# Eight blocks keep their GELU output instead of six, spread over the second pass; stored blocks are loaded into tiles that are already used

## The chip, the cores and the metric

The kernel runs on one core of one Trainium2 chip. The metric is the device time of one execution in microseconds (us). Before the change three runs gave 1454.07, 1455.67 and 1457.65 us: a median of 1455.67.

## The reference

A ConvNeXt-V2 block on one image of 512 x 512 pixels with 96 channels (C), in bf16: a depthwise 3x3 convolution, a normalisation over channels, a product up to 384 channels (E), GELU, a global response normalisation (GRN) whose scale needs the sum of squares of every one of the 384 channels over the whole image, and a product back to 96 channels with the input added.

```python
xp = jnp.pad(x, ((0,0),(pad,pad),(pad,pad),(0,0)))
out = jnp.zeros_like(x)
for i in range(K):
    for j in range(K):
        out = out + xp[:, i:i+H, j:j+W, :] * dw[i, j][None, None, None, :]
h = _layernorm(out, axis=-1)
h = jnp.einsum('bhwc,ce->bhwe', h, w1)
h = _gelu(h)
gx = jnp.sqrt((h * h).sum(axis=(1, 2), keepdims=True) + 1e-6)
nx = gx / (gx.mean(axis=-1, keepdims=True) + 1e-6)
h = grn_gamma * (h * nx) + grn_beta + h
h = jnp.einsum('bhwe,ec->bhwc', h, w2)
return x + h
```

The sums over the whole image split the work into two passes: the scale of the second product is known only when the GELU of every pixel has been seen once.

## The kernel before

**Blocks.** The image is cut into 128 blocks of 4 rows (`NBLK`). A block's GELU output g has 2048 pixels by 384 channels, 1.5 MB, in four quads of 512 pixels; one quad is turned out by one ScalarE GELU of 128 x 1536 from three PSUM banks (`banks3` gives two such sets in turn, so PE can be one quad ahead).

**Phase 1** takes the blocks in order: convolution (PE), statistics and normalisation, the normalised block `yn` to DRAM and back into a ring of six tiles `ynT`, then the first product and GELU, and the squares of g for the GRN sums. Up to block 113 the convolution of later blocks runs beside that; blocks 114 to 127 (`TAIL0` on) are turned out alone, by `mlp_tail` (L677), one after another.

The squares are taken in two ways. A quad in channel layout (`cm_unit`, three matmuls with the weights standing, channels on partitions) is squared by three VectorE statistics (`entry`, BATCH_NORM_STATS2 of 128 x 512). A quad in pixel layout (`px_unit`, pixels on partitions) is squared on PE: each half quad gives six gram matmuls of 128 x 128, g against itself, whose diagonal is added up. Grams are queued in a list and handed out by `gram_next` after each quad, one or two half quads at a time, so they run some quads later than the GELU they read. `cm_quads` says how many quads of a block take the first way. Only g in channel layout can be used by the second product.

**How phase 2 gets a block's g.** Four kinds of blocks:

- stored (`whole`, 35 of them): all four quads in channel layout, g written to DRAM in phase 1 and loaded again in phase 2 into one of two tiles `gl`
- held (`HELD`, six: 114, 116, 118, 120, 122, 125): all four quads in channel layout, g simply stays on chip
- `KEPT` (123, 124, 126, 127): recomputed, their `ynT` is still in the ring
- the others: recomputed; `ynT` is loaded again with three DMAs of 128 KB on SP's queue

So 87 blocks are recomputed (`made_q`): 12 matmuls of 128 x 512 and four GELUs each, into one of three tiles `gr`.

**Where the tail's g lies.** Held blocks 114 to 122 take the five tiles of the pool `g`, 125 the tile `gh`. Of the others, 115 to 124 go by turns into two views, `overs`, laid over the input tiles (`xin`) and the transposed input tiles (`xt`) of the convolution, which are used up by then; 126 and 127 go into `gr`.

**Between the phases** the last grams and statistics are summed, VectorE works out the scale and multiplies it into W2 (`W2s`), while the first quads are already being recomputed.

**Phase 2** goes through `ORDER`. `stage_mm2` makes a block's second product in four sub-tiles: 12 matmuls of 128 x 96 each, then VectorE adds the bias from PSUM, and after every second sub-tile the input `xr`. After each sub-tile `pace` (L372) issues recompute matmuls for blocks ahead: at least what the sub-tile after next reads, else an even share with a lead of `LEAD` = 6 quads, never more than three tiles `gr`, and never beyond the five blocks (`PRE`) whose loads have been issued.

```python
soon = (n, sub + 2) if sub < NSUB - 1 else (n + 1, 1)
due = sum(1 for v in todo if v < soon or v[0] < n)
even = LEAD + (n * NSUB + sub + 1) * total / (NSUB * NBLK)
advance(max(due, even), n + PRE)
```

At the start of block n, `load_xr` (POOL's queue) asks for the input of block n + 4 and `load_rest` for what block n + 5 needs: `ynT` on SP's queue, stored g on POOL's. Outputs leave on SP's queue, a block later. The order begins (K kept in the ring, H held, W stored, r recomputed)

```
K123 K124 K126 H114 K127 r1 W0 r2 r4 H116 r5 r6 W3 r8 r9 H118 r11 r12 W7 ...
```

and ends `... W110 r119 r121 W113`; the held blocks are at places 3, 9, 15, 21, 28 and 34.

Of the kernel before, what the change touches and what calls it, by code (L numbers as in the profile page):

```python
# [12 lines left out]
GR = 4  # L13
# [2 lines left out]
NEWTON_ITERS = 2  # L16
FILL = (6, 15)
BATCH = 4
NHELD = 6
WHOLE = (0, 3, 7)  # L20
NTAIL = 14
GRB = 3
# [34 lines left out]
def kernel(  # L57
# [25 lines left out]

    QW = GR * 128
    NQ = GR * W // QW
# [2 lines left out]
    r_dram = dram.tile([NBLK, GR, W], bf16, name="r_dram")  # L88

    TAIL0 = NBLK - NTAIL  # L90
    HELD = [NBLK - 6 - 2 * i for i in range(NHELD - 1)][::-1] + [NBLK - 3]
    KEPT = [NBLK - 5, NBLK - 4, NBLK - 2, NBLK - 1]

    def is_held(q):
        return q in HELD

    def is_whole(q):
        return q < TAIL0 and q % 10 in WHOLE
# [8 lines left out]
    whole = [q for q in range(NBLK) if is_whole(q)]  # L107
    g_dram = dram.tile([len(whole), 128, NQ * NCH * QW], bf16, name="g_dram")
# [4 lines left out]
    PXP = GR * W // 128  # L113
    MB = W // PXP
# [18 lines left out]
    consts = ctx.enter_context(tc.tile_pool(name="consts", bufs=1))  # L133
# [3 lines left out]
    dw9 = consts.tile([9, C], bf16, name="dw9")  # L137
    eye32 = consts.tile([128, 32], bf16, name="eye32")
    rowsel = consts.tile([128, GR], bf16, name="rowsel")
    w1_raw = consts.tile([C, E], bf16, name="w1_raw")  # L140
    w1p = consts.tile([128, E], bf16, name="w1p")
    w1s = consts.tile([128, E], bf16, name="w1s")
    Wq = consts.tile([128, NI, 3, GR, 32], bf16, name="Wq")
    w2_sb = consts.tile([128, NCH, C], bf16, name="w2_sb")
    gam_bf = consts.tile([128, NCH], bf16, name="gam_bf")
    bet_bf = consts.tile([128, NCH], bf16, name="bet_bf")
# [13 lines left out]
    NYT = 6  # L160
# [3 lines left out]

    W2s = consts.tile([128, NCH, C], bf16, name="W2s")
    B2c = consts.tile([128, C], f32, name="B2c")
    free = [[q for q in range(NBLK) if is_whole(q)], list(HELD)]
    free = [v for i, q in enumerate(free[0]) for v in (free[1][i:i + 1] + [q])]
    made_q = KEPT + [q for q in range(NBLK) if not is_whole(q) and not is_held(q) and q not in KEPT]
    ORDER = []  # L170
    for i, q in enumerate(made_q):
        ORDER.append(q)
        while len(ORDER) - i - 1 < (i + 1) * len(free) // len(made_q):
            ORDER.append(free[len(ORDER) - i - 1])
    assert sorted(ORDER) == list(range(NBLK))
    nth_made = {q: n for n, q in enumerate(made_q)}
    SLOTS = [q % NYT for q in KEPT + [NBLK - 6, NBLK - 3]]

    class late:
        pass  # L180
# [2 lines left out]
    pspool = ctx.enter_context(tc.tile_pool(name="ps", bufs=1, space=bass.MemoryType.PSUM))  # L183
    PS = pspool.tile([128, 8, W], f32, name="PS")
    p2 = ExitStack()
    SL = PXP + 2
    with ExitStack() as p1:
        pe, dve, act, pool, sp = (InOrder(tc, e) for e in (nc.tensor, nc.vector, nc.scalar, nc.gpsimd, nc.sync))
        bstpool = p1.enter_context(tc.tile_pool(name="bst", bufs=2))
# [19 lines left out]
            return PS[:, 7 - out_banks[0] % 2, :GPS * C].rearrange("p (g c) -> p g c", g=GPS)  # L209

        Y3 = PS[:, 4:7, :]
        pc = p1.enter_context(ExitStack())
        xinpool = pc.enter_context(tc.tile_pool(name="xin", side="right", bufs=1))
        xin_all = xinpool.tile([128, 4, SL, C], bf16, name="xin")
        xins = {}

        def shift(h, j):
# [21 lines left out]
        g_setup = gpool.tile([128, NQ, NCH, QW], bf16, name="g")[:].rearrange("p t j w -> p (t j w)")  # L239
        Wd = g_setup[:, :NI * 9 * 32].rearrange("p (i k c) -> p i k c", i=NI, k=9)  # L240
        dwx = g_setup[:9, NI * 9 * 32:NI * 9 * 32 + NI * GR * 32].rearrange("p (i q c) -> p i q c", i=NI, q=GR)
        zrow = consts.tile([128, W], bf16, name="zrow")
        dve.memset(zrow[:], 0.0)
        warm = consts.tile([32, 32], bf16, name="warm")
        dve.memset(warm[:], 0.0)
# [1 line left out]
        for b in range(min(2, NBLK)):  # L247
# [3 lines left out]
                       in_=zrow[:, None, :NI * GR * 32].to_broadcast([128, 3, NI * GR * 32]), func=ACTF.Identity)  # L251
# [4 lines left out]
        for q in range(GR):  # L256
            dve.tensor_copy(out=eye32[32 * q:32 * q + 32, :], in_=ident_f[32 * q:32 * q + 32, 32 * q:32 * q + 32])

        cen = consts.tile([C, 128], bf16, name="cen")
        xtpool = pc.enter_context(tc.tile_pool(name="xt", side="right", bufs=1))  # L260
        ypool = pc.enter_context(tc.tile_pool(name="ybf", side="right", bufs=13))
        ysqpool = pc.enter_context(tc.tile_pool(name="ysq", side="right", bufs=3))
        small = pc.enter_context(tc.tile_pool(name="small", side="right", bufs=2))
        rtpool = pc.enter_context(tc.tile_pool(name="rt", side="right", bufs=2))
        rbcpool = pc.enter_context(tc.tile_pool(name="rbc", side="right", bufs=3))
        ynpool = pc.enter_context(tc.tile_pool(name="yn", side="right", bufs=3))
        NXT = 5
        xt_ring = []
        xt_all = xtpool.tile([128, NXT, NI, SL * MB], bf16, name="xT")
        for i in range(NXT):  # L270
            xt_ring.append(xt_all[:, i])
        assert NXT * NI * SL * MB >= NQ * NCH * QW
        assert 4 * SL * C >= NQ * NCH * QW
        overs = [v.rearrange("p a b c -> p (a b c)")[:, :NQ * NCH * QW].rearrange("p (t j w) -> p t j w", t=NQ, j=NCH)
                 for v in (xt_all[:], xin_all[:])]
        NS = BATCH * GR * NG
        cap = 2048 // (C * 4)
# [1 line left out]
        NSUB = PXP // GPS  # L279

        def load_xr(n, pq):
            q = ORDER[n]
            r0 = q * GR
            xr = late.xr.tile([128, PXP, C], bf16, name="xr")
            pq.dma_start(out=xr[:], in_=x[0, r0:r0 + GR].rearrange("r w c -> (r w) c").rearrange(  # L285
                "(p g) c -> p g c", g=PXP))
            grp.setdefault(q, {})["xr"] = xr

        def load_rest(n, sq, pq):
            q = ORDER[n]  # L290
            v = grp.setdefault(q, {})
            if is_held(q):
                v["g"] = gs[q]
            elif is_whole(q):
                v["g"] = late.gl.tile([128, NQ, NCH, QW], bf16, name="gl")
                pq.dma_start(out=v["g"][:].rearrange("p t j w -> p (t j w)"), in_=g_dram[whole.index(q)])
            else:
                ynt = yn_ring[SLOTS[nth_made[q] % NYT]]
                if q not in KEPT:
                    read_spread(sq, ynt, q)  # L300
                v["ynt"], v["w1"] = ynt, w1p if q in KEPT else w1s

# [54 lines left out]
        PRE = 5  # L357
        XPRE = 4
        LEAD = 6
        todo = [(n, t) for n in range(NBLK) if ORDER[n] in nth_made for t in range(NQ)]  # L360
        total = len(todo)
        made, used = [0], [0]
# [9 lines left out]
        def pace(n, sub):  # L372
            soon = (n, sub + 2) if sub < NSUB - 1 else (n + 1, 1)
            due = sum(1 for v in todo if v < soon or v[0] < n)
            even = LEAD + (n * NSUB + sub + 1) * total / (NSUB * NBLK)
            advance(max(due, even), n + PRE)

        SG = PS[:, 7, :]
# [286 lines left out]
        gs = {}  # L665
# [9 lines left out]
            dve.bn_stats(out=bsts[k][:, j, e, :], in_=gs[b][:, m, j, :])  # L675

        def mlp_tail(b, get):  # L677
            if b == HELD[-1]:
                gs[b] = late.gh.tile([128, NQ, NCH, QW], bf16, name="gh")[:]
            elif is_held(b) or b < HELD[0]:  # L680
                gs[b] = gpool.tile([128, NQ, NCH, QW], bf16, name="g")[:]
            elif b > HELD[-1]:
                gs[b] = late.gr.tile([128, NQ, NCH, QW], bf16, name="gr")[:]
            else:
                overs.append(overs.pop(0))
                gs[b] = overs[0]
# [124 lines left out]
        for k, (b0, n) in enumerate(BATCHES):  # L811
# [16 lines left out]
            for b in range(b0, b0 + n):  # L828
# [4 lines left out]
                m = s + (3 if ramp else 4)  # L833
# [10 lines left out]
        for s in range(last_slot + 1):  # L844
# [71 lines left out]
            else:  # L916
                b = mlp[0]
# [57 lines left out]
            if s == last_slot - 3:  # L975
                pc.close()
                late.gr = p2.enter_context(tc.tile_pool(name="gr", side="right", bufs=GRB))
                late.gh = p2.enter_context(tc.tile_pool(name="gh", side="right", bufs=1))
                late.xr = p2.enter_context(tc.tile_pool(name="xr", side="right", bufs=5))
                late.gl = p2.enter_context(tc.tile_pool(name="gld", side="right", bufs=2))  # L980
                late.o = p2.enter_context(tc.tile_pool(name="o", side="right", bufs=6))
            if s == last_slot - 2:
                for n in range(XPRE):
# [52 lines left out]
    with p2:  # L1036
        def out_part(q, o_sb, v):
            r0 = q * GR
            nc.sync.dma_start(
                out=out[0, r0:r0 + GR].rearrange("r w c -> (r w) c").rearrange("(p g) c -> p g c", g=PXP)[:, v],  # L1040
                in_=o_sb[:, v])

        held = None
        FIRST = 8
        for n, q in enumerate(ORDER):
            sq, pq = (sp, pool) if n < FIRST else (nc.sync, nc.gpsimd)
            if n + XPRE < NBLK:
                load_xr(n + XPRE, pq)
            if n + PRE < NBLK:
                load_rest(n + PRE, sq, pq)  # L1050
            if n == NBLK - 1:
                stage_out(*held)
                held = None
            o_sb = stage_mm2(n, q)
            if held:
                stage_out(*held)
            held = (q, o_sb)
# [30 lines left out]
```

## Time and profile before

| | |
|---|---|
| median of the three runs | 1455.67 us |
| the profiled execution, its own time | 1458.11 us |
| its span in the trace | 1456.3 us |
| granted TensorE clock, mean | 0.995 |
| ScalarE busy | 1399.4 us, 96% |
| PE matmul busy | 1388.1 us, 95% |
| VectorE busy | 1317.4 us, 90% |
| GpSimd (POOL) busy | 901.7 us, 62% |
| data moved by DMA | 421.26 MB |
| first GELU of block 115 | 881.48 us |
| last GELU of block 127 begins (row of eight from 940.62) | about 950 us |
| last GELU of phase 2 ends | 1446.84 us |

PE is TensorE's matmuls, PEld its weight loads, DVE is VectorE, ACT is ScalarE, POOL is GpSimd, SP issues DMAs. A row of the timeline gives start and length in us, engine, line, operation, what is written from what (partitions x elements), and how many such instructions are merged; in brackets how long the engine had been idle and what ended that. Almost every instruction carries line 35, that of a helper which records the instructions, so rows are told apart by their tiles: `PS<-ynT,w1s` is recompute, `PS<-W2s,...` the second product, `bst<-...` a statistic, `PS<-xin` with 128 x 128 a gram. [...]

### The profile page before, as it was taken

How to read it: one execution, taken by the hardware profiler on the slowest of the kernel's cores; microseconds unless marked ns; L12 is line 12 of the kernel's file. 1: busy time of each engine (PE TensorE's matmuls, PEld its weight loads, DVE VectorE, ACT ScalarE, POOL GpSimd, SP SyncE). 2: the span in 40 equal slices, each digit the busy share in tenths (PEclk: the TensorE clock that was granted, in tenths of full speed). 3: DMA queues.
4: the chain of work that ended last, by engine and by line, in shares of the span. 5: the costliest groups of instructions: out<-in, count | busy, mean ns of one | idle time of the engine just before them, and what ended most of it. 6: DMA issues, size and time to landing. Idle time of an engine off the chain costs nothing.

```text
span 1456.3 us, 54718 instructions
## 1 busy us (share of the span) xinstructions
PE 1388.1 (95%) x23128; PEld 812.0 (56%) x23128; DVE 1317.4 (90%) x2422; ACT 1399.4 (96%) x1591; POOL 901.7 (62%) x796
## 2 busy tenths in 40 slices
PE   8889999999999999999999998899999999999998
PEld 3444444444444444444444445567777677777776
DVE  7749999999999999999999998778888788888887
ACT  6879999999999999999999999999999899999997
POOL 2559999999999999999899998201111111111110
PEclk9999999999999999999999999999999999999999
DMA  6478889898888988988889876649999999999997
GB/s 195 153 216 234 251 262 278 265 265 260 266 258 270 269 255 269 274 252 267 248 271 274 247 242 204 185 174 371 363 336 368 394 379 415 386 412 413 405 415 307
DMA packets 167275, 421.26 MB, mean 289 GB/s; under 512 B 34198, under 2 KB 83798, under 8 KB 162550
## 3 DMA queue, kind: packets, MB, share of 16 engines
q1 hardware_dynamic: 151508, 313.80, 67.5%
q0 software_dynamic: 14960, 103.82, 18.5%
q8 instruction: 181, 2.97, 0.9%
q14 instruction: 64, 0.52, 0.1%
q10 hardware_dynamic: 562, 0.15, 0.0%
HBM read 261.38 MB, written 156.22 MB: 287 GB/s over the span
## 4 chain that ended last, share of the span: by engine, by line
PE 37%; DVE 36%; ACT 10%; DMA 8%; POOL 4%; issue 3%; SPq 1%; ACTq 0%; POOLq 0%; DVEq 0%
PE PS L35 37%; DVE bst L35 26%; DVE xT L35 7%; ACT g L35 5%; DMA ynT<-yn_dram 3%; DMA yn_dram<-yn 2%; DMA out_dram<-o_sb 2%; ACT y_bf L35 2%; POOL yn L35 2%; ACT gr L35 1%; SPq L35 1%; DVE y_bf L35 1%; POOL ysq L35 1%; DVE o_sb L35 1%; ACT xT L35 1%
## 5 line engine op out<-in xcount | busy, mean ns | idle before, releaser
L35 ACT ACTIVATE g<-PS 128x512 bf16<-128x512 f32 (+2 forms) x1046 | 707.7, 835 | 10.3 <-PE PS L35 6.5
L35 DVE BATCH_NORM_STATS2 bst<-g 128x6 f32<-128x512 bf16 x1086 | 659.0, 672 | 23.5 <-ACT g L35 23.3
L35 ACT ACTIVATE gr<-PS 128x1536 bf16<-128x1536 f32 x356 | 493.1, 1451 | 13.1 <-PE PS L35 8.0
L35 POOL TENSOR_TENSOR yn<-y_bf,rbc 128x1536 bf16<-128x1536 bf16 x126 | 391.3, 3107 | 48.8 <-ACT rbc L35 23.3
L35 PE MATMUL PS<-xT,Wq 64*32 64x511 bf16 (+1 forms) x9198 | 346.1, 389 | 16.8 <-ACT y_bf L35 4.5
L35 PE MATMUL PS<-ynT,w1p 128*128 128x512 bf16 x1170 | 335.4, 382 | 25.4 <-ACT g L35 5.4
L35 DVE TENSOR_TENSOR o_sb<-PS,B2c 128x384 bf16<-128x384 f32 x512 | 280.6, 556 | 70.1 <-PE PS L35 63.6
L35 POOL TENSOR_TENSOR ysq<-y_bf 128x1536 bf16<-128x1536 bf16 x114 | 313.3, 2748 | 26.0 <-ACT y_bf L35 17.8
L35 PE MATMUL PS<-ynT,w1s 128*128 128x512 bf16 x996 | 269.1, 379 | 5.5 <-DMA ynT<-yn_dram 3.3
L285 POOL DMA_DIRECT2D xr<-in_x_dram x116 | 62.2, 537 | 297.9 <-DVE o_sb L35 297.9
L35 PEld LDWEIGHTS <-gr 128*128 128x128 bf16 x4248 | 208.7, 98 | 56.4 <-issue 0.7
L35 PE MATMUL PS<-W2s,gr 128*128 128x96 bf16 x4176 | 218.8, 206 | 0.5 <-DVE o_sb L35 0.4
L35 PEld LDWEIGHTS <-Wq 64*32 64x32 bf16 x9216 | 113.4, 90 | 179.8 <-issue 135.1
L35 ACT ACTIVATE y_bf<-PS 128x1536 bf16<-128x1536 f32 (+2 forms) x135 | 182.4, 1357 | 18.2 <-PE PS L35 18.1
L35 PEld LDWEIGHTS <-w1p 128*128 128x128 bf16 x1170 | 90.4, 98 | 181.1 <-issue 111.5
L35 DVE STREAM_TRANSPOSE xT<-xin 128x576 f32<-128x576 f32 (+1 forms) x256 | 181.5, 748 | 6.5 <-PE PS L35 6.5
L35 DVE TENSOR_TENSOR o_sb<-o_sb,xr 128x768 bf16<-128x768 bf16 x256 | 142.8, 558 | 8.9
L35 PEld LDWEIGHTS <-g 128*128 128x128 bf16 (+1 forms) x1611 | 98.7, 98 | 84.8 <-issue 54.8
L35 PE MATMUL PS<-w1p,ynT 128*128 128x256 bf16 (+2 forms) x828 | 125.8, 272 | 9.7 <-ACT g L35 2.7
L35 PE MATMUL PS<-g 128*128 128x128 bf16 x1368 | 115.3, 221 | 1.2 <-DVE PS L35 1.2
L35 PEld LDWEIGHTS <-w1s 128*128 128x128 bf16 x996 | 79.5, 98 | 46.0 <-issue 5.5
L35 PEld LDWEIGHTS <-gl 128*128 128x128 bf16 x1680 | 82.5, 98 | 23.1 <-issue 0.9
(115 smaller groups left out, 754.9 us busy)
## 6 DMA issues: line engine op xcount, KB each, us to landing
xin<-in_x_dram SPq DMA_DIRECT2D x126, 432.0 KB
g_dram<-g SPq DMA_DIRECT2D x105, 512.0 KB
gl<-g_dram POOLq DMA_DIRECT2D x35, 1536.0 KB, 9.3
yn_dram<-yn SPq DMA_DIRECT2D x512, 96.0 KB
ynT<-yn_dram SPq DMA_DIRECT2D x128, 384.0 KB
out_dram<-o_sb SPq DMA_DIRECT2D x127, 384.0 KB
xr<-in_x_dram POOLq DMA_DIRECT2D x124, 384.0 KB, 7.5
ynT<-yn_dram SPq DMA_DIRECT2D x249, 128.0 KB
```

Source lines behind the costliest of these rows:

```text
L35: r = f(*a, **k)
L285: pq.dma_start(out=xr[:], in_=x[0, r0:r0 + GR].rearrange("r w c -> (r w) c").rearrange("(p g) c -> p g c", g=PXP))
```

## The change

- Held blocks are eight: 114, 115, 117, 118, 120, 121, 124 and 125. `KEPT` is 122, 123, 126, 127. 85 blocks are recomputed; 116 and 119 are the two of the tail that need `ynT` again.
- The two tiles `gl` are gone. The pools of the convolution's `xin` and `xt` tiles stay open to the end; some constants of the convolution move to a pool that closes with it.
- The tail's g: 114 lies over `xt`; 116, 119 and 121 lie over `xin`, one after another (121 stays); 115, 117, 118, 120 and 122 take tiles of `g`; 123 and then 124 take the tile of 122 (`gs[b] = gs[b - 1]`); 125 takes `gh`; 126 and 127 `gr`.
- A stored block is loaded into the tile of 114 or of 115, by turns. `user` names the block that must have been through the second product first; while it has not, the load is put off (`ahead`) to a later turn of the loop.
- Held blocks are spread over the order, which begins `K122 H114 K123 K126 H115 K127 r1 W0 r2 r4 W3 r5 r6 W7 ...` and ends `... r111 r112 W113 r116 r119 H125`; they are at places 1, 4, 25, 46, 67, 88, 109 and 127.
- The lead of `pace` falls in a straight line from 6 quads at the start to 3 (`LAST_LEAD`) at the end.

```diff
-    HELD = [NBLK - 6 - 2 * i for i in range(NHELD - 1)][::-1] + [NBLK - 3]
-    KEPT = [NBLK - 5, NBLK - 4, NBLK - 2, NBLK - 1]
+    HELD = [TAIL0 + i for i in (0, 1, 3, 4, 6, 7, 10, 11)]
+    KEPT = [NBLK - 6, NBLK - 5, NBLK - 2, NBLK - 1]
+    IN_XT, IN_XIN, IN_GH = TAIL0, TAIL0 + 7, TAIL0 + 11
...
-    free = [[q for q in range(NBLK) if is_whole(q)], list(HELD)]
-    free = [v for i, q in enumerate(free[0]) for v in (free[1][i:i + 1] + [q])]
+    free, rest = HELD[:2], HELD[2:]
+    for i, q in enumerate(whole):
+        free.append(q)
+        if (i + 1) * len(HELD[2:]) // len(whole) > len(HELD[2:]) - len(rest):
+            free.append(rest.pop(0))
+    assert not rest
...
-        while len(ORDER) - i - 1 < (i + 1) * len(free) // len(made_q):
+        while len(ORDER) - i - 1 < ((i + 1) * len(free) + len(made_q) // 2) // len(made_q):
...
             elif is_whole(q):
-                v["g"] = late.gl.tile([128, NQ, NCH, QW], bf16, name="gl")
-                pq.dma_start(out=v["g"][:].rearrange("p t j w -> p (t j w)"), in_=g_dram[whole.index(q)])
+                v["g"] = gs[HELD[in_order.index(q) % 2]]
+                pq.dma_start(out=v["g"].rearrange("p t j w -> p (t j w)"), in_=g_dram[whole.index(q)])
...
+        LAST_LEAD = 3
+        in_order = [q for q in ORDER if is_whole(q)]
+        user = {}
+        for i, q in enumerate(in_order):
+            user[ORDER.index(q)] = ORDER.index(HELD[i] if i < 2 else in_order[i - 2])
+        assert min(user) >= PRE
...
-            even = LEAD + (n * NSUB + sub + 1) * total / (NSUB * NBLK)
+            even = LEAD + (n * NSUB + sub + 1) * (total + LAST_LEAD - LEAD) / (NSUB * NBLK)
...
         def mlp_tail(b, get):
-            if b == HELD[-1]:
+            if b == IN_GH:
                 gs[b] = late.gh.tile([128, NQ, NCH, QW], bf16, name="gh")[:]
-            elif is_held(b) or b < HELD[0]:
+            elif b > IN_GH:
+                gs[b] = late.gr.tile([128, NQ, NCH, QW], bf16, name="gr")[:]
+            elif b == IN_XT:
+                gs[b] = g_xt
+            elif b == IN_XIN or b < IN_XIN and not is_held(b):
+                gs[b] = g_xin
+            elif b - 1 > IN_XIN and not is_held(b - 1):
+                gs[b] = gs[b - 1]
+            else:
                 gs[b] = gpool.tile([128, NQ, NCH, QW], bf16, name="g")[:]
-            elif b > HELD[-1]:
-                gs[b] = late.gr.tile([128, NQ, NCH, QW], bf16, name="gr")[:]
-            else:
-                overs.append(overs.pop(0))
-                gs[b] = overs[0]
...
-                late.gl = p2.enter_context(tc.tile_pool(name="gld", side="right", bufs=2))
...
+        ahead = []
         for n, q in enumerate(ORDER):
...
+            for m in [m for m in ahead if user.get(m, -1) < n]:
+                load_rest(m, sq, pq)
+                ahead.remove(m)
             if n + PRE < NBLK:
-                load_rest(n + PRE, sq, pq)
+                if user.get(n + PRE, -1) < n:
+                    load_rest(n + PRE, sq, pq)
+                else:
+                    ahead.append(n + PRE)
```

More of the change, by code (lines that the diff above doesn't have):

```diff
@@ L18 @@
 BATCH = 4
-NHELD = 6
 WHOLE = (0, 3, 7)
@@ L139 @@
     rowsel = consts.tile([128, GR], bf16, name="rowsel")
-    w1_raw = consts.tile([C, E], bf16, name="w1_raw")
+    SL = PXP + 2
+    NXT = 5
+    xin_all = ctx.enter_context(tc.tile_pool(name="xin", side="right", bufs=1)).tile(
+        [128, 4, SL, C], bf16, name="xin")
+    xt_all = ctx.enter_context(tc.tile_pool(name="xt", side="right", bufs=1)).tile(
+        [128, NXT, NI, SL * MB], bf16, name="xT")
+    pc = ctx.enter_context(ExitStack())
+    conv_consts = pc.enter_context(tc.tile_pool(name="convc", side="right", bufs=1))
+    w1_raw = conv_consts.tile([C, E], bf16, name="w1_raw")
     w1p = consts.tile([128, E], bf16, name="w1p")
     w1s = consts.tile([128, E], bf16, name="w1s")
-    Wq = consts.tile([128, NI, 3, GR, 32], bf16, name="Wq")
+    Wq = conv_consts.tile([128, NI, 3, GR, 32], bf16, name="Wq")
     w2_sb = consts.tile([128, NCH, C], bf16, name="w2_sb")
@@ L176 @@
     nth_made = {q: n for n, q in enumerate(made_q)}
-    SLOTS = [q % NYT for q in KEPT + [NBLK - 6, NBLK - 3]]
+    SLOTS = [q % NYT for q in KEPT + [NBLK - 4, NBLK - 3]]
     class late:
@@ L185 @@
     p2 = ExitStack()
-    SL = PXP + 2
     with ExitStack() as p1:
@@ L211 @@
         Y3 = PS[:, 4:7, :]
-        pc = p1.enter_context(ExitStack())
-        xinpool = pc.enter_context(tc.tile_pool(name="xin", side="right", bufs=1))
-        xin_all = xinpool.tile([128, 4, SL, C], bf16, name="xin")
         xins = {}
@@ L241 @@
         dwx = g_setup[:9, NI * 9 * 32:NI * 9 * 32 + NI * GR * 32].rearrange("p (i q c) -> p i q c", i=NI, q=GR)
-        zrow = consts.tile([128, W], bf16, name="zrow")
+        zrow = conv_consts.tile([128, W], bf16, name="zrow")
         dve.memset(zrow[:], 0.0)
@@ L257 @@
             dve.tensor_copy(out=eye32[32 * q:32 * q + 32, :], in_=ident_f[32 * q:32 * q + 32, 32 * q:32 * q + 32])
-        cen = consts.tile([C, 128], bf16, name="cen")
-        xtpool = pc.enter_context(tc.tile_pool(name="xt", side="right", bufs=1))
+        cen = conv_consts.tile([C, 128], bf16, name="cen")
         ypool = pc.enter_context(tc.tile_pool(name="ybf", side="right", bufs=13))
@@ L266 @@
         ynpool = pc.enter_context(tc.tile_pool(name="yn", side="right", bufs=3))
-        NXT = 5
         xt_ring = []
-        xt_all = xtpool.tile([128, NXT, NI, SL * MB], bf16, name="xT")
         for i in range(NXT):
@@ L273 @@
         assert 4 * SL * C >= NQ * NCH * QW
-        overs = [v.rearrange("p a b c -> p (a b c)")[:, :NQ * NCH * QW].rearrange("p (t j w) -> p t j w", t=NQ, j=NCH)
+        g_xt, g_xin = [v.rearrange("p a b c -> p (a b c)")[:, :NQ * NCH * QW].rearrange("p (t j w) -> p t j w", t=NQ, j=NCH)
                  for v in (xt_all[:], xin_all[:])]
```

## The prediction

> **What bounds the kernel now.** First the page's busy line of PE, then the busy table by stretches of 100 us, whole and for the two kinds of matmul alone (columns: stretch, its length, busy us and count of each engine, granted clock, DMA share, GB/s). Phase 2 runs from about 953 us to the end.
>
> ```profile
> PE 1388.1 (95%) x23128; PEld 812.0 (56%) x23128; DVE 1317.4 (90%) x2422; ACT 1399.4 (96%) x1591; POOL 901.7 (62%) x796
> ...
> 1000.00:1100.00 100.00, 100.00 (x1481) 74.80 (x1480) 85.39 (x159) 98.89 (x73) 16.08 (x30) 1.00 0.98 361
> 1100.00:1200.00 100.00, 97.03 (x1425) 72.05 (x1422) 82.59 (x153) 95.63 (x70) 17.68 (x33) 1.00 1.00 381
> 1200.00:1300.00 100.00, 98.61 (x1456) 73.49 (x1454) 83.88 (x155) 97.28 (x71) 18.22 (x34) 1.00 1.01 404
> 1300.00:1400.00 100.00, 99.92 (x1478) 74.58 (x1475) 85.16 (x158) 98.66 (x72) 18.77 (x35) 1.00 1.02 410
> ...
> 1300.00:1400.00 100.00, 57.53 (x214) 17.05 (x215) 0.00 (x0) 1.00 1.02 410
> ...
> 1300.00:1400.00 100.00, 65.15 (x1264) 0.00 (x0) 1.00 1.02 410
> ```
>
> PE and ScalarE both look full, so pitches must decide. The timeline at 1201 us (start, length, engine, operation, count):
>
> ```profile
> 1201.87 0.81 PE L35 MATMUL PS<-ynT,w1s 128*128 128x512 bf16 x3
> 1202.52 0.67 PE L35 MATMUL PS<-W2s,gl 128*128 128x96 bf16 x12
> 1203.03 0.81 PE L35 MATMUL PS<-ynT,w1s 128*128 128x512 bf16 x3
> ...
> 1162.29 0.81 PE L35 MATMUL PS<-ynT,w1s 128*128 128x512 bf16 x3 [2.08 <-DMA ynT<-yn_dram]
> ```
>
> From start to start, a recomputed quad (3 matmuls) takes 0.65 us, 0.216 each, and a sub-tile of the second product (12 matmuls) 0.51 us, 0.0425 each; the listed lengths overlap. In the stretch 1300 to 1400 that makes 214 x 0.216 + 1264 x 0.0425 = 99.9 us of 100: PE sets phase 2. The last row is its exception: PE waits for a block's normalised input.
>
> The end of phase 1 (blocks 114 to 127, from 876 to 951 us) is another matter; ScalarE, VectorE and PE timelines:
>
> ```profile
> 886.80 5.53 ACT L35 ACTIVATE g<-PS 128x1536 bf16<-128x1536 f32 x4
> 892.12 5.57 ACT L35 ACTIVATE xT<-PS 128x1536 bf16<-128x1536 f32 x4
> ...
> 924.31 5.62 ACT L35 ACTIVATE xin<-PS 128x1536 bf16<-128x1536 f32 x4
> ...
> 876.52 7.36 DVE L35 BATCH_NORM_STATS2 bst<-g 128x6 f32<-128x512 bf16 x12 [0.48 <-ACT g L35]
> 883.79 1.87 DVE L35 BATCH_NORM_STATS2 bst<-xin 128x6 f32<-128x512 bf16 x3
> ...
> 886.30 0.83 PE L35 MATMUL PS<-xin 128*128 128x128 bf16 x12
> 887.00 0.81 PE L35 MATMUL PS<-ynT,w1p 128*128 128x512 bf16 x3
> ...
> 891.03 0.81 PE L35 MATMUL PS<-ynT,w1p 128*128 128x512 bf16 x3 [0.20 <-ACT g L35]
> ```
>
> ScalarE turns out a block each 5.32 us (1.33 a quad) with no gap: it sets this stage. VectorE needs 7.27 us for a block that keeps g (12 statistics), 1.8 for another (3), and catches up because the two kinds alternate. ScalarE does the same shape at 1.33 us here, while phase 2 has a quad per 1.40 (72 rows touch a stretch of 100 us, 71 fit): there it has slack.
>
> **The change part by part.**
>
> *Two blocks fewer recomputed in phase 2* (87 to 85): 24 matmuls off PE, 24 x 0.216 = -5.2 us. ScalarE loses 8 x 1.33 = 10.6 us, hidden behind PE as just shown. Six loads of ynT (0.79 MB) go.
>
> *In their place 18 more statistics in phase 1's end.* Kept blocks now come in pairs (114, 115; 117, 118; 120, 121). Walking VectorE from its row: block 114 done 883.8, 115 at 891.1, moments 0.55, 116 at 893.4, 117 starts when its first GELU ends (892.12 + 1.45 = 893.6), with a transpose and an aggregation of 1.1 us ends 902.0, 118 909.2, 119 911.0, 120 918.3, 121 925.5, the first quad of 122 927.3. That lag was free before; now 122, 123 and 124 share one tile, so the first GELU of 123, ready at 924.31 as in the row, must wait for those statistics: +3.0 us. Behind it wait the three other GELUs of 123, PE (both PSUM halves full) and all later blocks. Ends: 0 (VectorE not late) and 4.6 (a lag 1.5 us longer).
>
> *The same shared tile on PE.* Grams are issued late. In the changed program's order six gram matmuls of 122 stand behind the fourth GELU of 123, and six of 123 behind each of the third and fourth GELU of 124, and wait for ScalarE there (another six, behind 125's first matmuls, wait for nothing new). These four half-quads read the newer block's values. PE, in order, then gives the next quad only afterwards: 0.1 for the release (PE's row at 891.03 against a GELU end of 886.80 + 2 x 1.33 + 1.45 = 890.91), 0.35 (twelve in 0.70), 0.65 for the quad, 0.2 to ScalarE's start, and 0.12 by which ScalarE's GELUs otherwise overlap (1.45 long, 1.33 apart): 1.4 us. Three of them: +4.2; ends 2 (0.65 each, only the quad shows) and 5. The chain to the scaled W2 starts from the last GELU, so nothing later absorbs this: phase 1's end +7.2.
>
> *Lead six to three.* A quad read by a sub-tile must be through ScalarE: 0.2 + 1.45 us after its matmuls. In the forced order (one sub-tile, one quad) a step costs PE 0.51 + 0.65 = 1.16 us, ScalarE 1.33, so a run of eight quads (two recomputed blocks, then one that is not) puts ScalarE 1.4 us behind. A lead of six hides that. By the pacing rule a quad is issued 3 to 8 sub-tiles ahead of its reader before, 1 to 5 in the last quarter afterwards. I take the debt as growing from nothing to 1.1 us over the last eleven runs: 11 x 0.55 = +6; ends 0 and 11 x 1.4 = 15.
>
> *The end.* Rows of ScalarE, PE and VectorE; after the last GELU (1446.84 us) PE waits for VectorE between sub-tiles:
>
> ```profile
> 1431.33 15.51 ACT L35 ACTIVATE gr<-PS 128x1536 bf16<-128x1536 f32 x11
> ...
> 1449.42 1.18 PE L35 MATMUL PS<-W2s,gl 128*128 128x96 bf16 x24 [0.34 <-DVE o_sb L35]
> 1452.92 0.56 DVE L35 TENSOR_TENSOR o_sb<-o_sb,xr 128x768 bf16<-128x768 bf16 x1
> ```
>
> Recompute now ends 6 sub-tiles before the end, not 9; of about 1.9 us of such PE idle, 1 goes (ends 0, 2). The last block in the order, 125, keeps g: a change meant to end on a recomputed block does not do so, and none of the sum rests on it.
>
> *Loads.* Stored g waits for a used tile as it did for one of two buffers; it is issued 4 to 5 blocks ahead (15 to 18 us) against a median landing of 9.3; the first two wait for blocks 114 and 115, second and fifth in the order. On POOL's queue at most one xr load more stands ahead of it, and the xr loads behind it are four blocks ahead (15 us, landing in 7.5). Every ynT load is issued five blocks ahead, but by the pacing rule its recompute starts 10 to 12 sub-tiles after the issue in the first third (12 to 16 before) and 15 to 18 at the end. Two recomputed blocks and a stored one move 4.7 MB in 11.3 us of PE, 417 GB/s, against the 410 of the row; kept blocks, now one in 21, give relief, where before all six came in the first 35. PE's idle before recompute matmuls was 5.5 us from 960 us on. I take -1; ends -5 and +6, the same idle once more.
>
> Sum: 7.2 - 5.2 + 6 - 1 - 1 = +6.0 us. On the profiled span: 1456.3 + 6.0 = 1462.3. The median of the runs is 1455.67, 0.6 under that span: **1461.7 us**.
>
> **The rivals.**
>
> *ScalarE is what bounds phase 2* (faster). For: 98.9% busy from 1000 to 1100, a quad each 1.40 us; against: 1.33 in phase 1's end, and PE's 99.9. It decides once a GELU costs ScalarE more than 11.3 / 8 = 1.41 us of its own there. If so 8 x 1.40 = -11.2, the lead's +6 is none (PE would have time to run ahead), end and loads -2, phase 1's end +7.2: -6.0, 1449.7. [...]
>
> *The waits hide* (no change). A lead of three is enough, since over a whole run ScalarE has 10.6 us of work to PE's 11.3: 7.2 - 5.2 - 1 - 1 = 0.0, 1455.7. Against: the run's debt is local.
>
> *Transfers late early on* (slower still). Ten sub-tiles of 0.94 us are 9.4 us, about what a load needs when stored g is in front of it; 14 early blocks 0.45 us late each give +6 in place of -1: +13, 1468.7. Against: late loads showed only 5.5 us so far.
>
> **How the numbers follow.** Three tenths of a per cent (4.4 us) is about what this measurement tells from no change. Forecast 0.48, no change 0.24, ScalarE 0.17, transfers 0.11. Unknown ends added (tail 2 to 9.6, lead 0 to 15) and the cases outside: 1452 to 1467.5 leaves out most of ScalarE's case and half of the transfers'. The forecast's own range is 1457 to 1466, with a little of it under 1460. Faster 0.17, the same 0.27, slower 0.56.
>
> **What would show it.** In the changed profile: the GELU groups of 122 to 125 with a ScalarE gap of about 3 us waiting for VectorE statistics at 123, and three of 1.4 waiting for PE; the end of phase 1 7 us later; then phase 2 from the first product matmul to the end about 1 us shorter, with PE idle before products waiting for ScalarE's gr in the last 100 us. Wrong: no gap at 123, or phase 2 more than 5 us shorter or longer.

## The result, and the profile after

The changed kernel takes 1466.54 us (median of six runs, 1463.39 to 1473.16), the kernel before in the same comparison 1455.05 us (six runs, 1452.59 to 1457.65): a ratio of 1.0083, 95% interval 1.0060 to 1.0106. It is slower, by 11.5 us; the forecast was +6.0, to 1461.7 us. The time lies inside the whole range of 1452 to 1467.5, and 0.5 us above the forecast's own range of 1457 to 1466.

The two profiled executions differ by less, 1466.38 - 1458.11 = 8.3 us, because the profile of before is 3.1 us above its median. By stages (first GELU of block 114, first matmul of the second product, end of the span):

| us | before | after | difference | predicted |
|---|---|---|---|---|
| up to the first GELU of 114 | 875.04 | 872.90 | -2.1 | 0 |
| phase 1's end, up to the first product | 84.19 | 93.91 | +9.7 | +7.2 |
| phase 2 | 497.08 | 497.79 | +0.7 | -1.2 |
| span | 1456.31 | 1464.60 | +8.3 | +6.0 |

The first row is where the profile of before was long: in the twelve other profiles of this document that GELU starts between 870.0 and 872.9 us, the two that keep the order of before (e4 and e9) included. Nothing of the change is in it.

**Phase 1's end.** ScalarE's timeline of the changed kernel, from the last quads of 122 to 126 (start, length, engine, operation, count, and in brackets the idle time before and what ended it), then VectorE's and PE's rows that end its gaps:

```profile
917.39 5.57 ACT L34 ACTIVATE g<-PS 128x1536 bf16<-128x1536 f32 x4
925.22 4.19 ACT L34 ACTIVATE g<-PS 128x1536 bf16<-128x1536 f32 x3 [2.26 <-DVE bst L34]
929.88 1.45 ACT L34 ACTIVATE g<-PS 128x1536 bf16<-128x1536 f32 x1 [0.47 <-PE PS L34]
932.63 4.14 ACT L34 ACTIVATE g<-PS 128x1536 bf16<-128x1536 f32 x3 [1.30 <-PE PS L34]
938.61 1.45 ACT L34 ACTIVATE g<-PS 128x1536 bf16<-128x1536 f32 x1 [1.84 <-PE PS L34]
942.31 1.45 ACT L34 ACTIVATE gh<-PS 128x1536 bf16<-128x1536 f32 x1 [2.25 <-PE PS L34]
944.17 4.14 ACT L34 ACTIVATE gh<-PS 128x1536 bf16<-128x1536 f32 x3 [0.41 <-PE PS L34]
948.18 10.87 ACT L34 ACTIVATE gr<-PS 128x1536 bf16<-128x1536 f32 x8
...
916.12 7.21 DVE L34 BATCH_NORM_STATS2 bst<-xin 128x6 f32<-128x512 bf16 x12
923.23 1.87 DVE L34 BATCH_NORM_STATS2 bst<-g 128x6 f32<-128x512 bf16 x3
...
926.72 1.15 PE L34 MATMUL PS<-w1p,ynT 128*128 128x384 bf16 x6 [2.56 <-ACT g L34]
931.39 0.51 PE L34 MATMUL PS<-g 128*128 128x128 bf16 x6 [1.60 <-ACT g L34]
931.73 0.81 PE L34 MATMUL PS<-ynT,w1p 128*128 128x512 bf16 x3
936.82 0.51 PE L34 MATMUL PS<-g 128*128 128x128 bf16 x6 [1.88 <-ACT g L34]
937.16 1.35 PE L34 MATMUL PS<-ynT,w1p 128*128 128x512 bf16 x3
```

Before, ScalarE had no gap from 877 to 951 us. Now the first GELU of 123 (925.22) starts when VectorE has finished the first quad of 122 (923.23 + 1.87 = 925.10). The gaps of 1.30, 1.84 and 2.25 us stand where the grams wait for a GELU and the next quad behind them on PE. They are not alike: at 931.73 a quad's three matmuls take 0.81 us, at 937.16 1.35. The table by stretches (busy us and count of PE, PEld, DVE, ACT, POOL, then the granted clock) says why:

```profile
920.00:940.00 20.00, 11.95 (x99) 7.49 (x98) 12.42 (x21) 14.13 (x11) 2.06 (x2) 0.85 0.72 225
940.00:960.00 20.00, 16.15 (x139) 10.64 (x140) 15.19 (x36) 16.39 (x13) 0.00 (x0) 0.90 0.07 24
...
1300.00:1400.00 100.00, 99.76 (x1469) 73.63 (x1468) 85.98 (x159) 96.42 (x70) 17.75 (x33) 1.00 1.01 396
```

TensorE's clock is granted at 0.85 and 0.90 there (before: 1.00 in both). The trace has the clock at a half for 3.4 us from 927.1 and for 6.8 us from 937.3, each time after PE had been waiting for GELUs (2.56 us, then 1.60 and 1.88 in the rows above). Adding up, with 0.12 us for the overlap of neighbouring GELUs that each gap loses: VectorE 2.26, PE 0.47 + 1.30 + 1.84 + 2.25 + 0.41 = 6.27, one more of 0.45 at block 117, and 7 x 0.12 = 0.84: 9.8 us, against the 9.7 of the table.

**Phase 2.** The last line above is the one to set against before's: PE 99.76 of 100 us, as full as it was, ScalarE down from 98.66 to 96.42. The larger waits for `gr` lie after it. The changed kernel's timeline in the last 35 us:

```profile
1430.86 0.68 PE L34 MATMUL PS<-W2s,gr 128*128 128x96 bf16 x12 [0.66 <-ACT gr L34]
...
1456.46 0.68 PE L34 MATMUL PS<-W2s,gr 128*128 128x96 bf16 x12 [0.66 <-ACT gr L34]
...
1458.86 1.18 PE L34 MATMUL PS<-W2s,gh 128*128 128x96 bf16 x24 [0.39 <-DVE o_sb L34]
```

A product waits for a GELU output that ScalarE has only just turned out. The listed lengths of matmuls overlap (above, the six grams from 931.39 with their 0.51 us end at 931.90, and the next row starts at 931.73), so the bracket shows less than is lost; counted from start to start (what goes beyond 0.0425 us after a product matmul or 0.2157 after a recompute one, where it is more than 0.05 us), phase 2 divides into:

| us of phase 2 | before | after | difference | predicted |
|---|---|---|---|---|
| PE's work (what is left) | 487.26 | 482.84 | -4.4 | -5.2 |
| idle before a recompute matmul (late `ynT`) | 7.95 | 6.40 | -1.6 | -1 |
| idle before a product matmul (`gr` late) | 0 | 6.88 | +6.9 | +6 |
| idle after the last recompute matmul | 1.87 | 1.68 | -0.2 | -1 |

### The profile page after: what moved, and what is told of

It is laid out like the page before. It is cut to its first block, busy times and chain, and to the rows that moved or that the text cites. A ratio compares the mean times of both kernels' runs of the same rounds, so it can differ in the third digit from the quotient of the medians.

```text
span 1464.6 us, 54486 instructions
## 1 busy us (share of the span) xinstructions
PE 1384.6 (95%) x23014; PEld 802.6 (55%) x23014; DVE 1328.1 (91%) x2440; ACT 1392.4 (95%) x1583; POOL 902.3 (62%) x796
## 4 chain that ended last, share of the span: by engine, by line
PE 35%; DVE 35%; ACT 12%; DMA 12%; issue 3%; POOL 2%; SPq 1%; ACTq 0%; DVEq 0%; POOLq 0%
PE PS L34 35%; DVE bst L34 25%; ACT g L34 7%; DVE xT L34 6%; DMA ynT<-yn_dram 5%; DMA out_dram<-o_sb 4%; ACT y_bf L34 3%; ACT gr L34 2%; DMA rbc<-r_dram 2%; SPq L34 1%; DMA yn_dram<-yn 1%; POOL yn L34 1%; DVE y_bf L34 1%; DVE o_sb L34 1%; DVE mom L34 1%
## 5 line engine op out<-in xcount | busy, mean ns | idle before, releaser
L34 ACT ACTIVATE g<-PS 128x512 bf16<-128x512 f32 (+2 forms) x1054 | 718.3, 838 | 17.5 <-PE PS L34 11.8
L34 ACT ACTIVATE gr<-PS 128x1536 bf16<-128x1536 f32 x348 | 485.3, 1451 | 22.9 <-PE PS L34 16.5
L34 PE MATMUL PS<-ynT,w1p 128*128 128x512 bf16 x1188 | 342.7, 384 | 31.3 <-ACT g L34 7.4
L34 PE MATMUL PS<-ynT,w1s 128*128 128x512 bf16 x972 | 262.6, 379 | 4.9 <-DMA ynT<-yn_dram 4.5
L34 PEld LDWEIGHTS <-gr 128*128 128x128 bf16 x4152 | 202.7, 98 | 62.7 <-ACT gr L34 11.9
L34 PE MATMUL PS<-W2s,gr 128*128 128x96 bf16 x4080 | 214.2, 206 | 3.4 <-ACT gr L34 3.2
L34 PEld LDWEIGHTS <-g 128*128 128x128 bf16 (+1 forms) x2499 | 144.0, 98 | 104.1 <-issue 55.8
L34 ACT ACTIVATE y_bf<-PS 128x1536 bf16<-128x1536 f32 (+2 forms) x135 | 182.2, 1355 | 14.3 <-PE PS L34 14.2
L34 PE MATMUL PS<-w1p,ynT 128*128 128x384 bf16 (+2 forms) x792 | 121.9, 273 | 9.5 <-ACT g L34 4.7
L34 PE MATMUL PS<-g 128*128 128x128 bf16 x1440 | 121.9, 222 | 6.4 <-ACT g L34 5.1
L34 PEld LDWEIGHTS <-ynT 128*128 128x128 bf16 x792 | 61.5, 98 | 31.7 <-issue 14.3
```

Of the source, the lines that this page charges most:

```text
L34: r = f(*a, **k)
```

## The experiments

All times are medians, set against runs of the kernel before on the same chip (1455.05 us for the changed kernel, 1454.61 for e1 to e4, 1454.81 for e5 to e7, 1456.44 for e8 to e11). Stages and idle times are of one profiled execution each. Idle times are counted as in the table above.

| run | time, us | ratio to before, 95% interval | phase 1's end | phase 2 | idle before recompute | before product |
|---|---|---|---|---|---|---|
| after | 1466.54 | 1.0083, 1.0060 to 1.0106 | 93.91 | 497.79 | 6.4 | 6.9 |
| e1_prompt_grams | 1463.28 | 1.0056, 1.0029 to 1.0082 | 88.21 | 502.76 | 10.3 | 7.1 |
| e2_own_tile | 1460.53 | 1.0030, 1.0003 to 1.0057 | 84.54 | 503.30 | 10.7 | 7.1 |
| e3_lead_six | 1465.03 | 1.0076, 1.0047 to 1.0104 | 92.30 | 498.77 | 14.2 | 0.6 |
| e4_before_lead_three | 1515.77 | 1.0404, 1.0352 to 1.0455 | 83.54 | 560.88 | 6.6 | 53.9 |
| e5_pe_filler | 1465.65 | 1.0066, 1.0039 to 1.0092 | 91.14 | 498.82 | 7.4 | 6.9 |
| e6_pairs_apart | 1450.55 | 0.9970, 0.9945 to 0.9995 | 83.20 | 493.74 | 7.6 | 1.2 |
| e7_lead_even | 1460.60 | 1.0024, 0.9994 to 1.0053 | 91.98 | 487.24 | 2.1 | 0.9 |
| e8_pairs_apart_six_three | 1462.13 | 1.0036, 1.0012 to 1.0060 | 84.54 | 503.58 | 11.3 | 6.9 |
| e9_before_lead_even | 1466.68 | 1.0069, 1.0046 to 1.0091 | 82.37 | 508.45 | 0.4 | 16.7 |
| e10_pairs_apart_lead_four | 1448.64 | 0.9953, 0.9929 to 0.9978 | 83.26 | 491.86 | 5.8 | 1.1 |
| e11_lead_even_again | 1454.65, one run | | 91.95 | 489.60 | 4.5 | 0.9 |

### What lengthened phase 1's end

**Grams without delay.** In the changed kernel, blocks after 121 hand out two half quads of grams at a time:

```diff
-                gram_next(2 if len(grams) > 4 else 1)
+                gram_next(2 if len(grams) > 4 or b > IN_XIN else 1)
```

> From block 122 on, two half quads of grams are issued after every quad, so no gram of 122 or 123 stands behind a GELU that overwrites its tile. Theory (three gram waits, lengthened by a halved TensorE clock, make most of phase 1's end): the ScalarE gaps before the first and last quad of 124 and the first of 125 (1.30, 1.84 and 2.25 us in the changed profile) go, the wait for VectorE at 123 (2.26) stays; from the first GELU of block 114 to the first product matmul 93.9 falls to 87 to 88.5, the time by 5.5 to 7 below the changed kernel's 1466.5. Rival (the 18 more statistics and the pairs of kept blocks cost it, not the shared tile): nothing changes by more than 1 us.

The stage took 88.21 us, 5.7 less, as expected; the time fell by 3.3 us only, since phase 2 of the profiled run waited longer for its loads. ScalarE's timeline of this run at 123 and 124:

```profile
922.17 5.48 ACT L34 ACTIVATE g<-PS 128x1536 bf16<-128x1536 f32 x4 [2.25 <-DVE bst L34]
928.49 1.45 ACT L34 ACTIVATE g<-PS 128x1536 bf16<-128x1536 f32 x1 [0.84 <-ACT g L34]
930.21 4.13 ACT L34 ACTIVATE g<-PS 128x1536 bf16<-128x1536 f32 x3 [0.27 <-PE PS L34]
```

VectorE's wait is unchanged to a hundredth, the three waits for PE are gone but for 0.84 + 0.27 us: the order of the grams made them. What is left follows VectorE's wait: the trace has TensorE's clock at a half for 3.4 us from 925.7, and the quad that is late by 0.84 us is made in that time.

**No tile shared at that place.** Block 123 writes into 118's tile, so that the g of 118 is lost, and 124 into 122's:

```diff
-            elif b - 1 > IN_XIN and not is_held(b - 1):
-                gs[b] = gs[b - 1]
+            elif b == IN_XIN + 2:
+                gs[b] = gs[IN_XIN - 3]
+            elif b == IN_XIN + 3:
+                gs[b] = gs[IN_XIN + 1]
```

> Block 123 is written over the tile of kept block 118 and 124 over that of 122, two blocks earlier; block 118's g is lost, so its product is computed from 123's. Every wait of the shared tile is gone, both VectorE's and the grams'. Theory: from the first GELU of 114 to the first product matmul 84 to 85.5 us as before the change (84.2), the time 9 to 10 below the changed kernel's 1466.5, about 1457. Rival (statistics and pairs): it stays at 90 or more. Compared with the run that only issues grams earlier, the difference (2.5 to 3.5 us) is VectorE's wait alone.

The stage took 84.54 us, against 84.19 before the change. One row of ScalarE covers blocks 122 to 124:

```profile
915.96 16.33 ACT L34 ACTIVATE g<-PS 128x1536 bf16<-128x1536 f32 x12
```

Twelve quads without a gap: 9.4 of the 9.7 us hang on the one tile shared by 122, 123 and 124. The time, 6.0 us lower, missed its 9 to 10: phase 2 was 5.5 us longer than in the changed kernel's profile, 4.3 of it in late `ynT` loads.

**PE kept busy.** The changed kernel with matmuls whose result nobody reads, ahead of the waits:

```diff
+    FILLER = {(IN_XIN + 2, 0): 38, (IN_XIN + 2, 3): 22, (IN_XIN + 3, 2): 22, (IN_XIN + 3, 3): 22}
...
+                for _ in range(FILLER.get((b, t), 0)):
+                    pe.matmul(PS[:, 6, :128], lhsT=ident_b[:], rhs=ident_b[:], start=True, stop=True)
```

> The changed kernel with 104 matmuls added on TensorE in phase 1's end (22 or 38 of 128 x 128, written to a scratch bank and read by nobody), at the quads of blocks 123 and 124 before which TensorE now stands idle waiting for ScalarE. Theory (the gram waits of this stage grew from the 1.4 us that the sum gave them because TensorE's granted clock halves after it idles there): kept busy, TensorE keeps clock 1.0 from 920 to 960 us, where the changed kernel's page shows 0.85 and 0.90, the gaps of ScalarE before 1.30, 1.84 and 2.25 us come back to about 1.4 each or less, and from the first GELU of 114 to the first product takes 91 to 92.5 us in place of 93.9; the time falls by 1.5 to 2.5 us. Rival (the clock isn't the cause, only the place of the grams in the order): the clock may be full again but the gaps stay within 0.2 us of theirs, or grow by the added matmuls, and the stage takes 93.5 to 96 us.

ScalarE's timeline of this run, then its table by stretches:

```profile
923.10 5.48 ACT L34 ACTIVATE g<-PS 128x1536 bf16<-128x1536 f32 x4 [2.25 <-DVE bst L34]
929.87 4.13 ACT L34 ACTIVATE g<-PS 128x1536 bf16<-128x1536 f32 x3 [1.30 <-issue]
935.32 1.45 ACT L34 ACTIVATE g<-PS 128x1536 bf16<-128x1536 f32 x1 [1.31 <-PE PS L34]
938.08 5.48 ACT L34 ACTIVATE gh<-PS 128x1536 bf16<-128x1536 f32 x4 [1.31 <-PE PS L34]
```

```profile
920.00:940.00 20.00, 17.06 (x210) 13.14 (x209) 12.62 (x22) 13.83 (x11) 0.00 (x0) 1.00 0.69 218
940.00:960.00 20.00, 14.79 (x133) 9.58 (x132) 15.76 (x54) 18.42 (x15) 0.00 (x0) 1.00 0.00 1
```

With more work for PE the clock stays at 1.00, the three gaps are 1.30, 1.31 and 1.31 us, those of 0.47 and 0.41 are gone, and the stage takes 91.14 us, 2.8 less. The theory holds for the stage. The time fell by 0.9 us where 1.5 to 2.5 were expected; phase 2 was 1.0 us longer, again in loads, and so small a difference is not told apart by these runs.

### What phase 2 gained and gave back

**Lead of six to the end.**

```diff
-        LAST_LEAD = 3
+        LAST_LEAD = 6
```

> The lead stays at six to the end; all else as in the changed kernel. Theory of the prediction (the falling lead costs 6 us, because products wait for ScalarE): PE's waits for gr before products go (about 7 us of them from 1340 us on), phase 2 shortens by 5 to 7 us, the time is 1460. Rival (a longer lead makes each recompute start nearer to its load): those waits go, but PE waits for ynT instead, some 6 to 9 us more in the second half; phase 2 changes by less than 3 us either way.

PE's waits in phase 2, by what ended them (total, times, longest), of the changed kernel and of this run:

```profile
PE PS L34 <- DMA ynT<-yn_dram: 4.5, 5, 1.5
PE PS L34 <- ACT gr L34: 3.2, 9, 0.7
```

```profile
PE PS L34 <- DMA ynT<-yn_dram: 10.7, 13, 1.9
```

The waits for `gr` are gone, and phase 2 is no shorter: recompute now runs further ahead of its readers, and so nearer to its loads, which are asked for five blocks ahead whatever the lead, and it waits for them instead, 14.2 us in place of 6.4. The theory is out, and the rival is right in kind. Of its 6 to 9 us more in the second half, where the leads differ most, 3.8 came (2.0 to 5.8); the other 4 us lie in the first half, where profiles of the falling lead also have anything from 4.4 to 9.1 us.

**The falling lead in the order of before.** `LAST_LEAD = 3` and its term in `even`, put into the kernel before:

```diff
-            even = LEAD + (n * NSUB + sub + 1) * total / (NSUB * NBLK)
+            even = LEAD + (n * NSUB + sub + 1) * (total + LAST_LEAD - LEAD) / (NSUB * NBLK)
```

> The kernel before with nothing changed but the lead, falling from six to three. Theory of the prediction (a debt of ScalarE in runs of eight quads): some 6 us slower than before, 1461. Rival (the order matters: before the change it starts with three recomputed blocks and stays up to one block, four quads, ahead of the straight line of the pacing rule, so that a lead of three means quads issued one sub-tile ahead of their reader for most of the phase): 1 us or more of PE waiting for ScalarE in each of the last 25 to 40 runs, 30 to 50 us slower, 1485 to 1505.

61 us more, beyond what either side allowed for; the rival, that it is the order that makes the lead bearable, is right in kind. Its row of product matmuls (busy us, mean ns, idle before and what ended it; the bracket idle is again less than the count from start to start, 53.9):

```profile
L35 PE MATMUL PS<-W2s,gr 128*128 128x96 bf16 x4068 | 221.8, 208 | 40.5 <-ACT gr L35 40.1
```

Besides the waits, PE's work is 11 us longer by the same count, and the trace has TensorE's clock at a half for 41 us in all between 1364 and 1511 us. The two orders differ in one thing that fits this: with 87 recomputed blocks to 41 others, the order before has three recomputed blocks in a row at five places, 25 blocks apart (123, 124, 126, then 19, 21, 22, then 44, 45, 46 and so on); with 85 to 43 there are never more than two. A lead that costs 54 us of waiting in the one costs 7 in the other.

**A lead in between,** 4.5 throughout, in the changed kernel, and the same kernel once more for a second profile:

```diff
-        LEAD = 6
-        LAST_LEAD = 3
+        LEAD = 4.5
+        LAST_LEAD = 4.5
```

> The changed kernel with the lead 4.5 quads throughout, in place of six falling to three; nothing else. Theory (the two waits pull in opposite directions: a small lead late in phase 2 has TensorE wait 7.7 us for ScalarE's gr, a large one starts recompute sooner after its loads are issued, and it waits 6.4 us for ynT with the falling lead and 14.2 with a lead of six): in between both stay below 3.5 us, phase 2 takes 489 to 492 us, the time is 1458 to 1461 us. Rival (the loads are bound by bandwidth and the lead only moves their lateness about): waits of 14 us in sum as before, phase 2 497 to 500 us, time 1464 to 1467.

> The kernel of e7 once more, for a second profile, since the profiled run of e7 (1451.67 us) was the shortest of its ten (median 1460.6). Theory (runs of one kernel differ by when the ynT loads land): phase 1 to the first GELU of 114 again 870 to 873 us, the stage after it 91 to 93 us, and nearly all of the difference between the two profiles in waiting for ynT in phase 2, 5 to 11 us where e7 has 2.1. Rival: the difference lies in phase 1, up to the first GELU of 114 (874 us or more).

Phase 2 took 487.24 and 489.60 us, its waits before the last recompute matmul 3.0 and 5.4 us in sum instead of 13.3 (waits view of the first one, 1.3 us for `ynT` and none for `gr`):

```profile
PE PS L34 <- DMA ynT<-yn_dram: 1.3, 3, 0.6
PE PS L34 <- DVE o_sb L34: 0.7, 2, 0.3
```

So the waits don't merely change places. The median, 1460.60 us, lies in the range of the theory, but both profiled executions (1451.67 and 1454.65 us) are shorter than it, and six of the ten runs lie between 1459.46 and 1463.63. The two profiles do differ by 2.4 us of loads in phase 2, as expected in kind (4.5 us of late loads in the second, where 5 to 11 were expected); what the longer runs have more of, neither shows, and it stays open.

**The same lead in the kernel before.**

```diff
-        LEAD = 6
+        LEAD = 4.5
```

> The kernel before with its constant lead of six made 4.5, nothing else. Theory (its order has long runs of recomputed blocks without one that isn't, which a lead of six covers and a falling one did not, so a smaller lead costs it gr waits and saves it little, since its loads are late by 8 us in all): gr waits of 4 to 10 us, phase 2 497 to 504 us, time 1455 to 1462 us. Rival (a middle lead serves any order): gr waits under 2 us, ynT waits halved, phase 2 490 to 494 us, time 1448 to 1451, and then the gain of e6 over the kernel before owes nothing to the change.

Late loads go from 7.95 to 0.4 us, but waits for `gr` come to 16.7 us, more than the theory's 4 to 10, in five groups some 98 us apart (964 to 990, 1062 to 1088, 1161 to 1187 us and on), which is as often as three recomputed blocks stand in a row. Its waits view, from 962 us on (bracket idle, again less than the count):

```profile
PE PS L35 <- ACT gr L35: 6.7, 22, 0.7
```

Time 1466.68 us, 10 more than before: of the two orders a lead of 4.5 serves only the new one, so what it gives there rests on the change.

### A version that beats both

**Pairs kept apart.** Held blocks 114, 115, 117, 118, 120, 122, 124, 125; grams two at a time; lead 4.5:

```diff
-    HELD = [TAIL0 + i for i in (0, 1, 3, 4, 6, 7, 10, 11)]
-    KEPT = [NBLK - 6, NBLK - 5, NBLK - 2, NBLK - 1]
-    IN_XT, IN_XIN, IN_GH = TAIL0, TAIL0 + 7, TAIL0 + 11
+    HELD = [TAIL0 + i for i in (0, 1, 3, 4, 6, 8, 10, 11)]
+    KEPT = [NBLK - 5, NBLK - 2, NBLK - 1]
+    IN_XT, IN_XIN, IN_GH = TAIL0, (TAIL0 + 2, TAIL0 + 5, TAIL0 + 8), TAIL0 + 11
+    SHARED = {TAIL0 + 9: TAIL0 + 7, TAIL0 + 10: TAIL0 + 7}
...
-        LEAD = 6
-        LAST_LEAD = 3
+        LEAD = 4.5
+        LAST_LEAD = 4.5
...
-            elif b - 1 > IN_XIN and not is_held(b - 1):
-                gs[b] = gs[b - 1]
+            elif b in SHARED:
+                gs[b] = gs[SHARED[b]]
...
-                gram_next(2 if len(grams) > 4 else 1)
+                gram_next(2 if len(grams) > 4 or b > IN_XIN[-1] else 1)
```

> A candidate against both kernels: eight blocks keep g, but as 114, 115, 117, 118, 120, 122, 124 and 125, so that VectorE gets a block without twelve statistics between them; 116, 119 and 122 write into the used xin tile, 121, 123 and 124 share one other tile; grams are issued two at a time towards the end, so that none waits behind the last blocks; and the lead of the recompute is 4.5 quads throughout, in place of six falling to three. Theory (phase 1's end was lost to one tile shared by three blocks, and phase 2's gain to two waits that pull the lead in opposite directions, ScalarE's gr when it is small and the ynT loads when it is large): from the first GELU of 114 to the first product 84 to 86 us (before 84.2, changed 93.9), phase 2 489 to 492 us (497.1 and 497.8), time 1446 to 1450 us. Rival (the loads are limited by bandwidth, so that the waits only change places): phase 2 497 to 502 us, time 1455 to 1461.

1450.55 us, 0.9970 of before, just above the theory's 1446 to 1450. Phase 1's end is back (83.20 us, below the expected 84 to 86), phase 2 at 493.74 lies between the two expectations, with late loads of 7.6 us left.

**The lead undone.** The same with six falling to three:

> The kernel of e6 with the changed kernel's lead back, six falling to three, and nothing else of it undone. Theory (the lead is what cost phase 2, the placing of the kept blocks what cost phase 1's end): first GELU of 114 to first product 83 to 85 us as in e6, phase 2 back to 498 to 502 us with 7 to 8 us of TensorE waiting for gr before products, most of it after 1380 us, time 1455 to 1459 us. Rival (in e6 it was the other order of blocks that made phase 2 shorter): phase 2 492 to 495 us, time 1449 to 1452.

Phase 2 went to 503.58 us and the time to 1462.13, both beyond the theory's ranges, with 6.9 us of waits for `gr` and 11.3 for loads. The rival is out: of what e6 gains over the changed kernel, about 10 us are the lead's. Phase 2 differs by 503.58 - 493.74 = 9.8 us; the medians differ by 11.6, but their runs of before by 1.6 the same way.

**A lead of four.**

> The kernel of e6 with a lead of 4 quads in place of 4.5. Theory (in e6 waiting for ynT is still 7.6 us and for gr 1.5, so the balance lies lower): ynT waits 3 to 6 us, gr waits 1.5 to 3, phase 2 489 to 493 us, time 1446 to 1450 us. Rival (four is where ScalarE's debt of a run of eight quads, 1.4 us, comes through): gr waits 5 us or more, phase 2 495 to 500 us, time 1452 to 1457.

1448.64 us, 0.9953 of before (0.9929 to 0.9978): the lowest of all, though these runs do not tell it from e6's 0.9970 (0.9945 to 0.9995). Time and phase 2 are in the theory's ranges. PE's waits in its phase 2:

```profile
PE PS L34 <- DMA ynT<-yn_dram: 3.3, 6, 1.4
PE PS L34 <- ACT gr L34: 1.1, 2, 0.8
PE PS L34 <- DVE o_sb L34: 0.4, 1, 0.4
```

Against the profile of before, its phase 2 is 497.08 - 491.86 = 5.2 us shorter and phase 1's end 0.9. Of the 5.2 us, 3.6 are PE's work, by the same count: there the two blocks that are no longer recomputed arrive in the time. Most of the rest is late loads (5.8 us in place of 7.95).

## Why the prediction was right, and where it was short

- **VectorE's wait at 123**: predicted 3.0, measured 2.26 + 0.12 us, in the place named. VectorE ended the quad 52.2 us after the first GELU of 114, as walked (52.3); ScalarE came 0.7 us later than walked, most of it from its wait of 0.45 us at 117.
- **Three gram waits of 1.4 us: the term that was mis-sized.** The mechanism is shown by e1, and at a full clock the size is right as well: three gaps of 1.31 with the 0.12 make 4.3 us, against 4.2 (e5). But the sum took PE's durations from rows at clock 1.00, and the clock was granted at 0.85 and 0.90 where PE waited, at 1.00 where other matmuls filled the waits (e5): the changed kernel's gaps became 0.47, 1.30, 1.84, 2.25 and 0.41, with their overlaps 6.9 us, 2.6 more than in e5. The predicted upper end for this part, 5 us, did not cover it.
- **Two blocks fewer**: -5.2 predicted, PE's work fell by 4.4. With the same 85 blocks it lies within 482.1 and 483.9 us in all variants of the changed kernel, however long they waited.
- **Lead six to three**: +6 predicted, +6.9 measured, 3.8 of it as single waits of 0.37 and 0.82 us from 1394 on, the rest in pieces of 0.1 to 0.2 us. The mechanism is as predicted, but what the sum made of it is not: it took the 6 us as what the falling lead costs against six, and with six to the end phase 2 is 1.0 us longer (e3). The step treated the lead as costing only at its low end. E3, e7 and e11 show two prices pulling in opposite directions: a lead of six costs 14 us of late loads in this order, four and a half costs 3 to 5 in all.
- **The end**: -1 predicted, -0.2 measured. VectorE's three waits became one, as said, but two waits for `gr` (0.37 and 0.82 us, the first of them counted in the +6.9) came in their place. Before the change recompute ended ten sub-tiles before the end, not nine as the prediction has it.
- **Loads**: -1 predicted, -1.6 measured in this profile. That this fits is luck: with the same falling lead in the new orders, five profiles show 6.4 to 11.3 us, and four of them run the same phase 2. The changed kernel's is the lowest. (The prediction's 5.5 us of before is the sum of the bracket idle; from start to start it is 7.95.)
- **What is left of the miss** (11.5 measured, 6.0 forecast): 2.5 us in phase 1's end, 1.9 in phase 2, and 1.1 from the baseline, whose profiled execution was 3.1 us above its median, 2.1 of it in the first row of the table.
- **ScalarE as the bound of phase 2** is refuted: PE is as full as before at 1300 to 1400 us while ScalarE falls to 96.42, and in e7 phase 2 shrinks by 10.6 us with all of ScalarE's work still in it, down to PE's 482.9 us of work and some waits. The prediction's count from start to start, 99.9 of 100 us for PE, judged right.
- **Waits that hide** fell with the changed kernel's 6.9 us of waits for `gr`. **Transfers late early on** did not come in the changed kernel; the nearest to them is a lead of six (e3), with 8.4 of its 14.2 us of late loads in the first half.

## What to carry to other kernels

When a tile is handed to a third user, list who still reads it on every engine, and walk the slowest reader's backlog: 18 statistics more on an engine with slack cost 9.7 us through one shared tile, and with other sharing 0.4 (e2) or nothing (e6). A lead between producer and consumer has two prices, the wait for the producer and the wait for its inputs; take both from the profile, and search between them again after each change of order, since a lead that suits one order need not suit another: 4.5 gave 16.7 us of waits for `gr` with runs of three recomputed blocks, and 0.9 with runs of two.

## What the hardware showed that was not expected

TensorE's clock went to a half in a stage where PE's longest gap was 2.56 us: 3.4 us of it from 927.1 and 6.8 us from 937.3 in the changed kernel, 3.4 us from 937.7 in e3 and e7. In e7 the gaps in the ten microseconds ahead of it were of 1.88, 1.88 and 1.60 us; matmuls ran between them. In the 3.4 us just ahead of these four halvings, a stretch as long as the shortest of them, matmuls are busy for 0.85, 1.53, 1.16 and 1.33 us. Filling the waits with matmuls that nobody reads (e5), which left PE no gap above 0.65 us from 926 to 946, kept the clock at 1.00, though ScalarE still waited 1.30, 1.31 and 1.31 us.
